# Cluster products of q and k of a group as one piece in two PSUM banks, in a kernel that fuses routed attention with a SwiGLU layer

One Trainium2 chip, one of its cores. The metric is device time in microseconds (us) of one launch; lower is better. All runs that are compared here were at a granted TensorE clock of 0.997 to 1.0. PE is TensorE, DVE VectorE, ACT ScalarE, POOL GpSimd.

## The reference, cut to what matters

```python
def _attn_ref(q, k, v, centroids):             # (4, 8, 768, 64) each; 16 centroids per head
    ...                                        # q_n, k_n, c_n: rows divided by their norms
    q_assign = np.argmax(np.einsum('bhsd,hcd->bhsc', q_n, c_n), axis=-1)
    k_assign = np.argmax(np.einsum('bhsd,hcd->bhsc', k_n, c_n), axis=-1)
    mask = q_assign[:, :, :, None] == k_assign[:, :, None, :]
    scores = np.where(mask, scale * np.matmul(q, k.transpose(0, 1, 3, 2)), -1e9)
    return softmax(scores) @ v                 # written out in the original

def _moe_ref(x, w_gate, w_val, w_out, rms_g):  # x (3072, 512): the attention's output, heads side by side
    xn = x / rms * rms_g
    g = xn @ w_gate                            # (512, 1536)
    return (silu(g) * (xn @ w_val)) @ w_out
```

A query sees only keys of its own cluster. The kernel finds each row's cluster by a product with 16 normalised centroids (the *cluster product*), a maximum and a comparison, and appends the one-hot row of the cluster to q and to k, so that the score matmul itself adds the mask.

## The kernel before: the parts that matter

Work is cut into 8 *units* (half a batch's queries, 8 heads, three *gaps* per head, one after each pair of score matmuls) and 8 *groups* of 4 heads. While ScalarE and TensorE work on the scores of unit u, other work is put between: the SwiGLU products of earlier units and the preparation of a group (u + 2; unit 1 prepares groups 2 and 3). A SwiGLU step is a *gate* product and a *value* product on TensorE, a tanh on ScalarE, and two steps on VectorE (L366 after the gate, L370 after the value) that combine them and so free the two PSUM buffers. All of it goes through engines that take instructions in the program's order.

```python
    ps_s = pool("ps_s", 2, space=PSUM)     # scores, 2 buffers
    ps_a = pool("ps_a", 1, space=PSUM)     # attention output
    ps_g = pool("ps_g", 3, space=PSUM)     # everything else: gate, val, o, transposes, cluster products
...
    def cluster_steps(g, m, h0=0, h1=HG, early=False):       # m: 0 q, 1 k
        ...
        def products(): _products(g, m, h0, h1, early, of)
        def largest():  ...   # DVE: maximum over 16 clusters           (mx)
        def compare():  ...   # DVE: equal to the maximum, bf16         (ohT)
        def back():     ...   # DVE: transpose back to one-hot rows     (oh)
        return [products, largest, compare, back]

    def _products(g, m, h0, h1, early, of):
        ps = ... ps_g.tile([P, UQ], F32, tag="gen", name="sc")
        ...
        for h in range(h0, h1):            # four heads, 32 output columns each, fp32
            nc.tensor.matmul(ps[32 * h:32 * h + 32], lhsT=cblk[:, g * HG % H + h],
                             rhs=qkT[g, h // 2][:, h % 2, m], start=True, stop=True)
        sct = asg.tile([P, UQ], F32, tag="scT", name="scT", bufs=2)
        nc.vector.transpose(sct[r], ps[r])
...
    def group_work(g):
        ...
        a = []
        for m in range(2):
            a += [(0.0 if i else 0.7, f) for i, f in enumerate(cluster_steps(g, m))]
        a.append((0.0, lambda: [place(nc.gpsimd, g, m) for m in range(2)]))
...
    def attention(heads, fill, skip=0, ahead={}, hooks={}):
        gaps = [(u, h, i) for u, h in heads for i in range(UNITS[u][2])]
        total, done, n = sum(c for c, _ in fill), 0.0, 0
        for at, (u, h, i) in enumerate(gaps):
            scores(u, h, i)                # two matmuls into a ps_s buffer, exp on ACT out of it
            ...                            # at i == 1: the value product (acc) of the head before
            if h == H - 1:
                squares(u, i, False)       # ACT: sum of squares of heads 0 to 5, one third per gap of head 7
            ...
            while n < len(fill) and at >= skip and done <= total * (at + 1 - skip) / (len(gaps) - skip):
                done += fill[n][0]         # the cost in us that the author gave the step
                fill[n][1]()
                n += 1
```

With `skip` = 1 the first gap of a unit gets no fill, so that the last score of a unit and the first two of the next stand close together.

The softmax here doesn't subtract the row's maximum and nothing guards it: scores larger than these inputs give would overflow.

Of the kernel before, what the change touches and what calls it, by code (L numbers as in the profile page):

```python
# [22 lines left out]
def kernel(  # L23
# [60 lines left out]
    def load_qk(n):  # L84
        if n < B * H:
            load(n, 0)
            load(n, 1)

    def load_v(n, vq=None):
        if n >= B * H:  # L90
            return
        stagedv[n] = stage.tile([P, ST, D], F32, tag="vs", name="vs", bufs=NV)
        (vq or nc.sync).dma_start(out=stagedv[n], in_=src(v, n))
# [100 lines left out]
    def trans(g, h, part):  # L194
        if (g, h // 2) not in qkT:
            qkT[g, h // 2] = qk32.tile([P, 2, 2, UQ], F32, tag="qkT", name="qkT")
        qk = staged[g * HG + h]
        ps = ps_g.tile([P, UQ], F32, tag="gen", name="tq")
        for i in range(HT):
            nc.tensor.transpose(ps[:, i * P:(i + 1) * P], qk[:, part, 2 * i:2 * i + 2].rearrange("p t d -> p (t d)"),  # L200
                                ident_f)
        nc.scalar.copy(qkT[g, h // 2][:, h % 2, part], ps)  # L202

    def qcast(g, h, es=(0, 1)):
        for e in es:
            nc.gpsimd.tensor_copy(qext[g % 4][:D, h, e * UQ:(e + 1) * UQ], qkT[g, h // 2][e * D:(e + 1) * D, h % 2, 0])  # L206

    def kcast(g, h, on=None, es=(0, 1)):
        for e in es:
            to, of = kext[g % 4][:D, h, e * UQ:(e + 1) * UQ], qkT[g, h // 2][e * D:(e + 1) * D, h % 2, 1]  # L210
            if on is nc.scalar:
                nc.scalar.activation(to, of, ACT.Copy, scale=1.0 / ZS)
            else:
                (on or nc.vector).tensor_scalar_mul(to, of, 1.0 / ZS)  # L214

    def vcast(n):
        nc.gpsimd.tensor_copy(vbf[n // HG % 4][:, n % HG, :, :D], stagedv[n])
# [8 lines left out]
    def cluster_steps(g, m, h0=0, h1=HG, early=False):  # L226

        r = slice(32 * h0, 32 * h1)
        n = UQ // NC
        of = {}  # L230

        def products():
            _products(g, m, h0, h1, early, of)

        def largest():
            of["mx"] = small.tile([P, n], F32, tag="mx", name="mx")
            nc.vector.tensor_reduce(of["mx"][r], of["cl"], axis=AX, op=ALU.max)

        def compare():
            of["ohT"] = asg.tile([P, UQ], BF16, tag="ohT", name="ohT", bufs=2)  # L240
            nc.vector.tensor_tensor(of["ohT"][r].rearrange("p (n c) -> p n c", c=NC), of["cl"],
                                    of["mx"][r].unsqueeze(2).broadcast_to([32 * (h1 - h0), n, NC]), op=ALU.is_equal)

        def back():
            oh = asg.tile([P, UQ], BF16, tag="oh", name="oh", bufs=4)
            nc.vector.transpose(oh[r], of["ohT"][r])  # L246
            put[g, m, h0] = ((kext if m else qext)[g % 4], oh, h0, h1)

        return [products, largest, compare, back]

    def _products(g, m, h0, h1, early, of):
        ps = ps_s.tile([P, UQ], F32, tag="s", name="sc") if early else ps_g.tile([P, UQ], F32, tag="gen", name="sc")
        r = slice(32 * h0, 32 * h1)
        for h in range(h0, h1):
# [4 lines that stand above are left out]
        of["cl"] = sct[r].rearrange("p (n c) -> p n c", c=NC)  # L259
# [3 lines left out]
    def place(on, g, m, h0=0, es=(0, 1)):  # L263

        ext, oh, _, h1 = put[g, m, h0]
        for h in range(h0, h1):
            for e in es:
                on.dma_start(out=ext[D:D + NC, h, e * UQ:(e + 1) * UQ],  # L268
                             in_=oh[32 * h + e * NC:32 * h + (e + 1) * NC])
# [117 lines left out]
    def group_work(g):  # L387

        t, c = [], []
        for h in range(HG):  # L390
            n = g * HG + h
            t += [(0.3, lambda h=h: trans(g, h, 0)), (0.3, lambda h=h: trans(g, h, 1))]

            def casts(h=h, n=n):
                qcast(g, h)
                vcast(n)
                load_qk(n + NQ)
                load_v(n + NV)
                kcast(g, h, es=(0,))
            c += [(0.0, casts), (0.0, lambda h=h: kcast(g, h, es=(1,)))]  # L400
        a = []
        for m in range(2):
            a += [(0.0 if i else 0.7, f) for i, f in enumerate(cluster_steps(g, m))]
        a.append((0.0, lambda: [place(nc.gpsimd, g, m) for m in range(2)]))
        return t, c, a

    def group(g):
        t, c, a = group_work(g)
        return [x for h in range(HG) for x in t[2 * h:2 * h + 2] + c[2 * h:2 * h + 2]] + a
# [13 lines left out]
    def ffn_work(u):  # L423
        n = UNITS[u][2] / HT
        w = [(0.18 * n, lambda c=c: xtrans(u, c)) for c in range(CC)]
        for f in range(FC):
            for val in (False, True):
                w.append((0.64 * n, lambda f=f, val=val: gv(u, f, val)))
        return w

    def out_work(u):
        return [(0.86, lambda t=t, p=p: out_mm(u, t, p)) for t in range(UNITS[u][2]) for p in range(3)]
# [131 lines left out]
    for u in range(1, NU):  # L564
        ffn, o, g = ffn_work(u - 1), out_work(u - 2) if u > 1 else [], u + 2
        if u == 1:
            t, c, a = group_work(2)
            fill, head, prep = [], t, c + a + group(3)
        else:
            fill, head, prep = ffn_work(u - 2)[CUT:], [], group(g) if g < NG else []  # L570
        fill += [(0.0, lambda u=u: rms(u - 1))] + head
        fill += o[:-3] + ffn[:2] + o[-3:-2] + ffn[2:3] + o[-2:-1] + ffn[3:4] + o[-1:] + spread(ffn[CC:CUT], prep)
        attention([(u, h) for h in range(H)], fill, 1)
# [36 lines left out]
```

## Time and profile before

| | before |
|---|---|
| time, median of 3 runs | 361.62 us (361.56 to 361.79) |
| span of the profiled run | 359.7 us |
| busy: PE, ACT, DVE, POOL | 345.2, 256.1, 237.1, 110.2 us |
| two cluster pieces of a group on TensorE, each to the next start, with 0.09 us lost ahead of it | 2 x 0.875 us |

The prediction below shows the lines themselves. One thing helps in reading them: the bracket at the end of a timeline line ("idle before") tells whether the engine stood idle before that instruction, and for whom.

### The profile page before, as it was taken

To read this page: it belongs to the slowest core of one execution; us is meant where nothing else is said; L and a number is where in the kernel's file an instruction comes from. 1 tells how busy PE (TensorE), PEld (TensorE's weight loads), DVE (VectorE), ACT (ScalarE), POOL (GpSimd) and SP (SyncE) were. 2 spreads that over 40 slices of the span, in tenths; PEclk is the share of its full clock that TensorE was granted. 3 is DMA by queue.
4 is the path that set the end of the run, shared out by engine and by line. 5 is a ranking of instruction groups with operands and counts; after the bars stand their busy time and mean duration, and the time that the engine had idled before them with its cause. 6 is when DMAs were issued, how large, how long until landed. Compare 5 with 4: busy or idle time off the path is not lost.

```text
span 359.7 us, 8049 instructions
## 1 busy us (share of the span) xinstructions
PE 345.2 (96%) x3027; PEld 210.0 (58%) x3047; DVE 237.1 (66%) x577; ACT 256.1 (71%) x455; POOL 110.2 (31%) x221
## 2 busy tenths in 40 slices
PE   8999799999999999999999999999999999999995
PEld 4555455655575656755576556756566656654552
DVE  5994379596567874686667865687656575677332
ACT  5789977996588866887588865978668866861320
POOL 1699306896051801535033711327000000000000
PEclk9999999999999999999999999999999999999999
DMA  7549999962154102610130002001010001002002
GB/s 256 185 121 212 244 241 270 334 190 67 64 157 133 24 29 89 202 40 19 59 118 2 16 8 87 2 2 24 38 52 3 0 31 58 2 3 80 8 2 87
DMA packets 28039, 32.03 MB, mean 89 GB/s; under 512 B 4960, under 2 KB 24928, under 8 KB 28000
## 3 DMA queue, kind: packets, MB, share of 16 engines
q1 hardware_dynamic: 18352, 24.75, 21.6%
q0 software_dynamic: 9072, 5.98, 10.0%
q10 hardware_dynamic: 576, 0.79, 0.7%
q8 instruction: 24, 0.39, 0.4%
q14 instruction: 15, 0.12, 0.1%
HBM read 28.35 MB, written 6.29 MB: 96 GB/s over the span
## 4 chain that ended last, share of the span: by engine, by line
PE 71%; DVE 14%; ACT 8%; issue 3%; POOL 1%; DMA 1%; SPq 0%; DVEq 0%; ACTq 0%
PE gate L357 16%; PE val L357 16%; PE s L284 13%; PE o L379 12%; PE acc L302 8%; ACT pT L288 5%; PE tq L200 4%; DVE o_sb L382 2%; PE sc L255 2%; ACT xn L322 2%; DVE xn L334 1%; PE warm L112 1%; DVE th L366 1%; DVE kext L214 1%; DVE scT L258 1%
## 5 line engine op out<-in xcount | busy, mean ns | idle before, releaser
L288 ACT ACTIVATE pT<-s,off 128x768 bf16<-128x768 f32 x192 | 171.0, 902 | 50.2 <-PE s L284 49.1
L284 PE MATMUL s<-qext,kext 80*128 80x384 bf16 x384 | 93.5, 325 | 3.0 <-ACT pT L288 2.6
L357 PE MATMUL gate<-xnT,wg 128*128 128x384 bf16 x384 | 78.5, 325 | 0.2 <-DVE xnT L345 0.2
L357 PE MATMUL val<-xnT,wv 128*128 128x384 bf16 x384 | 78.1, 326 | 0.4 <-DVE th L366 0.3
L366 DVE SCALAR_TENSOR_TENSOR th<-th,gate 128x384 f32<-128x384 f32 x84 | 46.3, 552 | 44.0 <-ACT th L365 43.6
L379 PE MATMUL o<-wo,gvT 128*128 128x512 bf16 x272 | 68.8, 378 | 2.1 <-DVE o_sb L382 1.0
L206 POOL CAST qext<-qkT 64x384 bf16<-64x384 f32 x64 | 33.0, 524 | 93.7 <-ACT qkT L202 92.1
L284 PEld LDWEIGHTS <-kext 80*128 80x128 bf16 x384 | 37.0, 98 | 35.3 <-issue 7.7
L365 ACT ACTIVATE th<-gate 128x384 f32<-128x384 f32 x84 | 41.1, 489 | 15.8 <-PE gate L357 15.2
L357 PEld LDWEIGHTS <-wv 128*128 128x128 bf16 x384 | 36.1, 97 | 26.1 <-issue 4.5
L370 DVE SCALAR_TENSOR_TENSOR gvT<-th,val 128x384 bf16<-128x384 f32 x84 | 46.1, 548 | 7.4 <-PE val L357 2.3
L357 PEld LDWEIGHTS <-wg 128*128 128x128 bf16 x384 | 35.8, 97 | 24.5 <-issue 3.6
L302 PEld LDWEIGHTS <-pT 128*128 128x128 bf16 x1152 | 43.5, 97 | 9.3 <-ACT pT L288 0.6
L302 PE MATMUL acc<-vbf,pT 128*128 128x65 bf16 x1152 | 45.6, 193 | 0.5 <-ACT pT L288 0.5
L379 PEld LDWEIGHTS <-gvT 128*128 128x128 bf16 x288 | 27.0, 97 | 27.7 <-issue 2.0
L202 ACT COPY qkT<-tq 128x384 f32<-128x384 f32 x64 | 29.2, 488 | 5.9 <-PE tq L200 5.0
L200 PE MATMUL tq<-ident_f,qk 128*128 128x128 f32 x192 | 30.2, 280 | 1.6 <-ACT qkT L202 1.2
L268 POOL DMA_DIRECT2D qext<-oh x48 | 23.1, 490 | 24.5 <-DVE oh L246 24.3
L200 PEld LDWEIGHTS tq<-ident_f,qk 128*128 128x128 f32 x192 | 23.2, 143 | 8.7 <-ACT qkT L202 2.2
L214 DVE TENSOR_SCALAR kext<-qkT 64x384 bf16<-64x384 f32 x60 | 23.8, 396 | 2.3 <-ACT qkT L202 1.6
L382 DVE COPY o_sb<-o 128x512 f32<-128x512 f32 x24 | 16.4, 686 | 12.5 <-PE o L379 12.5
L268 POOL DMA_DIRECT2D kext<-oh x48 | 22.9, 485 | 2.4 <-DVE th L366 1.2
(63 smaller groups left out, 241.9 us busy)
## 6 DMA issues: line engine op xcount, KB each, us to landing
qk<-in_q_dram SPq DMA_DIRECT2D x32, 192.0 KB, 3.9
vs<-in_v_dram SPq DMA_DIRECT2D x32, 192.0 KB, 3.7
out_dram<-o_sb SPq DMA_DIRECT2D x24, 256.0 KB, 2.0
qk<-in_k_dram SPq DMA_DIRECT2D x28, 192.0 KB, 4.0
wg<-in_moe_w_gate_dram POOLq DMA_DIRECT2D x4, 384.0 KB, 12.4
wv<-in_moe_w_val_dram POOLq DMA_DIRECT2D x4, 384.0 KB, 14.8
wo<-in_moe_w_out_dram POOLq DMA_DIRECT2D x3, 512.0 KB, 24.7
kext<-oh POOLq DMA_DIRECT2D x52, 12.0 KB, 1.6
```

The lines of the kernel that those rows point to most:

```text
L200: nc.tensor.transpose(ps[:, i * P:(i + 1) * P], qk[:, part, 2 * i:2 * i + 2].rearrange("p t d -> p (t d)"), ident_f)
L202: nc.scalar.copy(qkT[g, h // 2][:, h % 2, part], ps)
L206: nc.gpsimd.tensor_copy(qext[g % 4][:D, h, e * UQ:(e + 1) * UQ], qkT[g, h // 2][e * D:(e + 1) * D, h % 2, 0])
L268: on.dma_start(out=ext[D:D + NC, h, e * UQ:(e + 1) * UQ], in_=oh[32 * h + e * NC:32 * h + (e + 1) * NC])
L284: nc.tensor.matmul(ps[:, j, :w] if nt == HT else flat[:, j * w:(j + 1) * w], lhsT=kext[g % 4][:KR, hh, kc * P:(kc + 1) * P], rhs=qext[g % ...
L288: nc.scalar.activation(pT[u, h][:, n * i:n * i + n, :w], of, ACT.Exp, bias=off, scale=scale * ZS)
L302: nc.tensor.matmul(acc[:, h % 2, t], lhsT=pT[u, h][:, kc, t * P:(t + 1) * P], rhs=vbf[g % 4][:, hh, kc % HT * 2 + kc // HT], start=kc == 0 ...
L357: nc.tensor.matmul(ps, lhsT=w[:, c, f * P:(f + 1) * P], rhs=xnT[u][:, c, :n], start=c == 0, stop=c == CC - 1)
L365: nc.scalar.activation(th, ps, ACT.Tanh, scale=0.5)
L366: nc.vector.scalar_tensor_tensor(th, th, 1.0, ps, op0=ALU.add, op1=ALU.mult)
L370: nc.vector.scalar_tensor_tensor(gvT[u][:, f, :n], gates[u], 0.5, ps, op0=ALU.mult, op1=ALU.mult)
L379: nc.tensor.matmul(outs[u], lhsT=gvT[u][:, f, t * P:(t + 1) * P], rhs=wo[:, f], start=f == 0, stop=f == FC - 1)
```

## The change

The two cluster pieces of a group (q, then k) each take TensorE into its 32-column mode (four products of 32 output columns side by side, in place of one that uses all 128 columns) and out again. The change issues both products in one piece, in two PSUM buffers, to pay for one such excursion per group. DVE's later steps stay single.

```diff
-        a = []
-        for m in range(2):
-            a += [(0.0 if i else 0.7, f) for i, f in enumerate(cluster_steps(g, m))]
+        q_steps, k_steps = (cluster_steps(g, m) for m in range(2))
+        a = [(1.4, lambda: (q_steps[0](), k_steps[0]()))] + [(0.0, f) for f in q_steps[1:] + k_steps[1:]]
         a.append((0.0, lambda: [place(nc.gpsimd, g, m) for m in range(2)]))
```

## The prediction

> **What bounds the kernel now.** I read the page first, then the engines' busy time by stretch, then TensorE's timeline around the cluster products (tile `sc`), then the chain of waits in the stretches where groups are prepared.
>
> The page, parts 1 and 4 (busy time, and the chain that ended last):
>
> ```profile
> PE 345.2 (96%) x3027; PEld 210.0 (58%) x3047; DVE 237.1 (66%) x577; ACT 256.1 (71%) x455; POOL 110.2 (31%) x221
> ...
> PE 71%; DVE 14%; ACT 8%; issue 3%; POOL 1%; DMA 1%; SPq 0%; DVEq 0%; ACTq 0%
> ```
>
> TensorE (PE) is busy 96% and carries 71% of the chain. So time taken off TensorE's stream shortens the run, unless it is taken where VectorE (DVE) or ScalarE (ACT) set the pace, and 22% of the chain is theirs. Where is that? The windows view answers for two stretches, first the one in which groups 2 and 3 are prepared (attention of unit 1), then a piece of unit 3, which stands for units 2 to 5 (groups 4 to 7, one each):
>
> ```profile
> 50.00:60.00 10.00, 9.91 (x96) 5.33 (x95) 9.46 (x22) 7.89 (x12) 3.01 (x6) 1.00 1.16 267
> 60.00:70.00 10.00, 9.67 (x110) 7.32 (x108) 6.81 (x17) 9.30 (x17) 8.39 (x17) 1.00 1.11 327
> 70.00:80.00 10.00, 9.70 (x98) 5.36 (x94) 9.05 (x19) 9.07 (x18) 9.13 (x19) 1.00 0.66 198
> ...
> 110.50:119.50 9.00, 9.00 (x90) 4.88 (x88) 7.49 (x17) 6.86 (x15) 2.87 (x7) 1.00 0.22 67
> ```
>
> The columns after the length are PE, weight loads, DVE, ACT and GpSimd. In unit 1 DVE has 9.46 of 10 us while the cluster steps of group 2 run and 9.05 while those of group 3 run, with ACT at 9.07: three engines are nearly full. In the later unit PE is full and DVE and ACT have a fifth free. The chain of waits, asked for these stretches alone, agrees: from 108 to 121 us every piece of it is PE; from 49.8 to 64.1 and from 71.5 to 80.3 us nearly every piece is DVE, ending in these two:
>
> ```profile
> 64.09 0.81 PE val L357 x4
> ...
> 80.35 0.81 PE val L357 x4
> ```
>
> Both are value products that waited for DVE's gate step to free a PSUM buffer.
>
> **What one piece of cluster products costs TensorE.** The timeline of PE in unit 3 (start us, duration, what); the ends of matmuls are modelled, so I use differences of starts only:
>
> ```profile
> 111.19 0.49 PE L284 MATMUL s<-qext,kext 80*128 80x384 bf16 x2
> 111.61 0.85 PE L255 MATMUL sc<-qkT,cblk 128*32 128x384 f32 x8
> 112.40 0.50 PE L357 MATMUL val<-xnT,wv 128*128 128x384 bf16 x2
> ```
>
> A score matmul of 384 columns holds PE about 0.163 us start to start (two in sequence 0.325), so the score pair ends its stream at 111.52. The cluster product starts at 111.61: about 0.09 us of nothing. Then the next matmul starts 0.79 us after it (0.785 in the records). The eight records are four 32-column products of two passes each; the second pass of a product follows the first at about 0.35, the four products of a pass within 0.02. Two passes of 384 columns[...] are 2 x 0.32 = 0.64 us. So one piece takes 0.09 + 0.785 = 0.875 us, of which about 0.23 is neither streaming nor anything else.
>
> **What the Trainium skill says.**
> - "TensorEngine Tiling (Array Packing)", Tiling Modes, Key Properties: "Changing tiling mode (not just tile) drains the TensorE". The cluster products are 128x32 tiles between 128x128 matmuls, so each piece has two such changes. The trace agrees in size: 0.09 us before, and about 0.1 us after the last stream.
> - "Perfetto Trace Analysis", Tensor Engine Instruction: the profiler's matmul end is computed, not observed. Agreed: PE's records overlap (0.49 us for two that take 0.325). Hence a "busy" of 9.00 of 9.00 does not mean that there is no idle time to win, and I count starts.
> - "Perfetto Trace Analysis", Optimizing Tensor Performance, Matmuls: independent groups should rotate through PSUM banks so that evacuation overlaps. Here three buffers rotate among transposes, gate, value and cluster products, and the change fills two of the three at once. The two waits at 64.09 and 80.35 show that this rotation already bites in unit 1.
>
> **The change, part by part.** Nothing is added or removed: the same eight cluster matmuls per group, the same transposes (0.57 us each), reductions, comparisons and transposes back on DVE. For groups 2 to 7 the products of k move up beside those of q, and the transposes of the two PSUM tiles stand back to back; the built order shows `sc x8` where `sc x4` stood twice, once in unit 2 to 5 each and twice in unit 1. Groups 0 and 1 are untouched.
>
> *Removed:* one entry and one exit of the tiled mode per group. The kernel before contains the merged form once already, in its prologue, where two half pieces follow each other directly:
>
> ```profile
> 11.28 0.38 PE L112 MATMUL warm<-kext 128*128 128x512 bf16 x1
> 11.59 1.48 PE L255 MATMUL sc<-qkT,cblk 128*32 128x384 f32 x8
> 13.01 0.55 PE L200 MATMUL tq<-ident_f,qk 128*128 128x128 f32 x3
> ```
>
> Next start minus first start is 1.42 us (1.415) for four passes; a lone half piece of two passes at 9.20 us takes 0.77. A second pair of passes thus costs 1.415 - 0.771 = 0.644 us: pure streaming. So the merged piece should take 0.785 + 0.644 + 0.09 = 1.52 us in place of 2 x 0.875 = 1.75: **0.23 us saved per group**.
>
> *Units 2 to 5 (4 groups):* is the saving kept? I walked the new order with the durations above, from the cluster piece's start at t = 0. Its q bank is written by about 0.75, its k bank by 1.4. DVE transposes them by about 1.4 and 2.1. The order of PE afterwards is two scores, gate, two scores, 18 of the `acc` products, value, gate, two scores, value. The gate at 1.75 needs the bank of the value product before the piece (freed about 0.6), the value at 3.4 needs the q bank (1.4), the gate at 4.1 the k bank (2.1), the next value at 5.1 needs the first gate's bank, freed by DVE's gate step at about 3.8. Every bank is free over a microsecond ahead, so no new wait. One small stall of the old kernel stays: in the old trace the value after the second piece starts at 117.59, 0.16 us late, and the third of four scores 0.07 late. That sum is set by ACT (tanh 0.49, then exp 0.9, before a score buffer is free), so freeing the value's bank earlier only moves it to the score. Saved: 4 x 0.23 = **0.92 us**, all on PE's path.
>
> *Unit 1 (2 groups):* the PE time is saved too, 2 x 0.23 = 0.46, but here DVE paces. The gate after the merged piece of group 2 reaches PE at about 55.24 and needs the bank that DVE frees at 55.43 (`gvT` at 54.89, 0.55 long), so it starts at about 55.48: a wait of 0.24 eats the saving. Later DVE does two transposes, a maximum and two gate steps in another order; by summing its steps from 55.73 I get the second gate step done at about 61.9 against 61.2 before, and the transposes of q that need its bank would wait some 0.5 us. The value that waited until 64.09 would then start between 63.8 and 64.4. For group 3 DVE and ACT are both full and the same set of DVE steps precedes the gate step that releases the value at 80.35. I set unit 1 at **0, give or take 0.5**.
>
> Sum: 361.62 - 0.92 - 0 = **360.7 us**, 0.25% less.
>
> **The rivals.**
> 1. *All of it arrives* (also in unit 1): 6 x 0.23 = 1.4, plus two small waits of the old order in group 2 that would vanish (0.13 before the second piece, 0.18 before a transpose): about 360.0. For it: PE is 97 to 99% busy in unit 1 as well, and DVE has some idle pieces there that the new order may fill. Against it: the chain there is DVE's.
> 2. *A PSUM wait takes the place of the switch.* Two of three buffers are held until two transposes of DVE are through, 1.1 us plus DVE's queue. If DVE lags by over a microsecond in the later units as well, each group gains a wait of 0.2 to 0.5 us: 361 to 362.5. For it: DVE is 83% busy in the window at 110.5, and its order is fixed. Against it: my walk leaves over a microsecond.
> 3. *ACT starves, then is late.* During 1.52 us no score is made, and afterwards four scores come close together (group 3). ACT has 24% free in the later unit and each exp takes 0.9; in unit 1 this could cost 0.5 once: 361.2.
> 4. *Off the path.* If the unit boundaries (exp, squares, then DVE's normalisation) set the time, nothing changes: 361.6. Against it: PE waits for almost nothing between 85 and 125.
>
> **Range and chances.** The core, 0.92, rests on a measured merged piece and is good to 0.15; unit 1 adds 0.5 either way, and rival 2 has perhaps one chance in seven. The runs before agree within 0.25 us. So 8 times in 10 the time is between 359.8 and 361.7. Two per cent would be 7.2 us; all the cluster products' own PE time in these groups is 6 x 1.75 = 10.5, so neither side is within reach: faster 0.01, same 0.98, slower 0.01.
>
> **What would show it.** Right: each merged piece has 16 records and the next matmul starts about 1.43 us after the first; from unit 2 to unit 5 the distance between the same score matmul of successive units shrinks by about 0.23; DVE, ACT and PE do as many instructions as before. In unit 1 a gate waits for `gvT` just after the piece, and a transpose of q some 4 us later. Wrong: a gap over 0.2 us on PE after the piece in units 2 to 5 with DVE's `scT` as releaser (rival 2), over 0.6 us gained in unit 1 (rival 1) or lost there (rivals 2 and 3), or a merged piece longer than 1.6 us, which would make the switch cheaper than I take it.

## The result, and the profile after

| | before | after |
|---|---|---|
| time, median of 4 runs each | 361.59 us | 362.25 us |
| span of the profiled run | 359.7 us | 360.3 us |

The ratio is 1.0029, 95% interval 1.0004 to 1.0053: not faster by 0.25% but slower by 0.3%. (A ratio here is the mean time of one kernel's fast runs over that of the other's of the same rounds, so not quite the ratio of the medians.) 362.25 lies above the predicted range, whose top was 361.7.

The page of the kernel after, parts 1 and 4:

```profile
PE 344.4 (96%) x3047; PEld 210.0 (58%) x3047; DVE 236.4 (66%) x577; ACT 256.2 (71%) x455; POOL 109.5 (30%) x221
...
PE 65%; ACT 11%; DVE 10%; DMA 6%; POOL 3%; issue 3%; SPq 0%; ACTq 0%; POOLq 0%; DVEq 0%
```

The work is the same (the 20 PE records more are some that the first trace had lost), but PE carries less of the chain and ACT more, 11% against 8%. That is the first hint.

The merged piece itself is what was forecast. PE's timeline in unit 2 (the stretch from 108 to 119 us that the prediction calls unit 3; counted by exps, three per head, it is the end of unit 2, and the reading is the same):

```profile
112.18 0.81 PE L357 MATMUL val<-xnT,wv 128*128 128x384 bf16 x4
112.92 1.50 PE L255 MATMUL sc<-qkT,cblk 128*32 128x384 f32 x16
114.36 0.50 PE L284 MATMUL s<-qext,kext 80*128 80x384 bf16 x2
```

The next matmul starts 1.43 us after the first of sixteen records, in all six merged pieces, and 0.09 us are lost ahead of it: 1.52 us, as worked out, and 0.23 less than two pieces. So the saving was made. Where did it go?

To find out I take the start of the exp of each head (the ACT instruction on L288) in both traces, count from the first exp of unit 1, and subtract:

| exp of (unit, head) | after minus before, us |
|---|---|
| 1,4 | -0.15 |
| 1,5 | +0.43 |
| 1,7 and 2,0 | +1.05, +1.04 |
| 2,2 to 2,6 | +1.05 |
| 2,7 | +1.72 |
| 3,0 | +1.01 |
| 4,0; 5,0; 6,0 | +1.00, +0.99, +0.98 |
| end of the run | +1.01 |

(Unit 1 itself starts at 40.11 us in one trace and at 39.69 in the other; the kernels are the same until there, and this start lay between 39.69 and 40.90 in the runs. That is as wide as the scatter of one kernel's times, 362.05 to 363.13 for the kernel after; counting from there takes it out of the comparison.)

So all of the loss, 1.04 us, arises in unit 1. In units 2 to 5 nothing is lost and next to nothing gained: 0.06 for four groups in place of 0.92. And in each of them the exp of head 7 is suddenly 0.68 later, and back by the next unit.

**Units 2 to 5.** ACT's timeline around head 7 of unit 2, before:

```profile
113.64 0.90 ACT L288 ACTIVATE pT<-s,off 128x768 bf16<-128x768 f32 x1 [0.97 <-PE s L284]
...
115.32 0.90 ACT L288 ACTIVATE pT<-s,off 128x768 bf16<-128x768 f32 x1
...
117.30 0.49 ACT L365 ACTIVATE th<-gate 128x384 f32<-128x384 f32 x1 [0.58 <-PE gate L357]
117.69 0.89 ACT L288 ACTIVATE pT<-s,off 128x768 bf16<-128x768 f32 x1
```

and after:

```profile
114.95 0.90 ACT L288 ACTIVATE pT<-s,off 128x768 bf16<-128x768 f32 x1 [1.62 <-PE s L284]
115.75 0.51 ACT L322 ACTIVATE xn<-x 128x384 bf16<-128x384 f32 x1
...
116.26 0.48 ACT L365 ACTIVATE th<-gate 128x384 f32<-128x384 f32 x1
116.63 0.90 ACT L288 ACTIVATE pT<-s,off 128x768 bf16<-128x768 f32 x1
...
117.91 0.49 ACT L365 ACTIVATE th<-gate 128x384 f32<-128x384 f32 x1
118.28 0.91 ACT L288 ACTIVATE pT<-s,off 128x768 bf16<-128x768 f32 x1
```

Read the brackets. Before, ACT stood idle 0.97 us ahead of head 7's first exp, and again 0.58 us ahead of a tanh: it kept up and waited for PE. After, it stands idle 1.62 us while PE does the merged piece, and from 114.95 on no line has a bracket: ACT works without a break through exp, squares (L322), tanh, exp, squares, tanh, exp. It is behind, and PE finds it so. PE's timeline, before and then after:

```profile
117.59 0.81 PE L357 MATMUL val<-xnT,wv 128*128 128x384 bf16 x4
118.23 0.88 PE L284 MATMUL s<-qext,kext 80*128 80x384 bf16 x4
```

```profile
117.85 0.81 PE L357 MATMUL val<-xnT,wv 128*128 128x384 bf16 x4
118.50 0.49 PE L284 MATMUL s<-qext,kext 80*128 80x384 bf16 x2
119.25 0.48 PE L284 MATMUL s<-qext,kext 80*128 80x384 bf16 x2 [0.26 <-ACT pT L288]
```

Four score matmuls in a row are the last score of unit 2 and the first of unit 3. The second pair needs a score buffer whose exp is not finished. By differences of starts (118.50 to 119.25, where two score matmuls take 0.325) PE loses 0.42 us there; before, it lost 0.07 there and 0.16 at the value product ahead. The account of a unit: 0.23 less for the mode, 0.16 less at the value, 0.35 more at the score, together -0.04; measured -0.01 to -0.03.

**Unit 1.** The windows view of the kernel after, for the three stretches that the prediction shows of before:

```profile
50.00:60.00 10.00, 9.68 (x96) 5.62 (x95) 9.73 (x23) 7.95 (x12) 3.49 (x7) 1.00 1.17 267
60.00:70.00 10.00, 9.24 (x107) 7.00 (x106) 6.92 (x16) 8.80 (x16) 8.36 (x17) 1.00 1.10 325
70.00:80.00 10.00, 8.90 (x93) 4.96 (x90) 8.07 (x18) 8.72 (x17) 9.50 (x20) 1.00 0.73 218
```

PE's busy time fell from 9.91, 9.67 and 9.70 of 10 us. Its timeline names what it waited for:

```profile
59.30 0.81 PE L357 MATMUL val<-xnT,wv 128*128 128x384 bf16 x4 [0.26 <-DVE gvT L370]
...
61.65 0.81 PE L357 MATMUL gate<-xnT,wg 128*128 128x384 bf16 x4 [0.31 <-DVE th L366]
...
64.22 0.81 PE L357 MATMUL val<-xnT,wv 128*128 128x384 bf16 x4 [0.45 <-DVE th L366]
...
77.58 0.48 PE L284 MATMUL s<-qext,kext 80*128 80x384 bf16 x2 [1.09 <-ACT pT L288]
```

Before, the last two were at 64.09 and 76.95, with brackets of 0.33 and 0.30; the first two have no counterpart. At group 2's piece PE waits for DVE to free PSUM buffers; group 3's loses time to ACT at the same kind of place as in the later units. There the merged piece holds back head 7's first score by 0.64 us, which is the second product's share of it (1.43 less 0.785). ACT's timeline of the kernel before shows why none of it was made good:

```profile
72.00 1.94 ACT L288 ACTIVATE pT<-s,off 128x768 bf16<-128x768 f32 x2 [0.51 <-PE s L284]
...
79.65 0.90 ACT L288 ACTIVATE pT<-s,off 128x768 bf16<-128x768 f32 x1 [0.28 <-PE s L284]
```

No line between these two has a bracket, and from 72.10 to 78.80 ACT is busy 6.56 of 6.70 us: in unit 1 it had next to no idle time in head 7 even before the change.

### The profile page after: what moved, and what is told of

The parts are those of the page before. It is cut to its first block, busy times and chain, and to the rows that moved or that the text cites. A ratio compares the mean times of both kernels' runs of the same rounds, so it can differ in the third digit from the quotient of the medians.

```text
span 360.3 us, 8076 instructions
## 1 busy us (share of the span) xinstructions
PE 344.4 (96%) x3047; PEld 210.0 (58%) x3047; DVE 236.4 (66%) x577; ACT 256.2 (71%) x455; POOL 109.5 (30%) x221
## 4 chain that ended last, share of the span: by engine, by line
PE 65%; ACT 11%; DVE 10%; DMA 6%; POOL 3%; issue 3%; SPq 0%; ACTq 0%; POOLq 0%; DVEq 0%
PE val L357 14%; PE gate L357 14%; PE o L379 12%; PE s L284 11%; ACT pT L288 7%; PE acc L302 7%; PE tq L200 4%; DMA vs<-in_v_dram 4%; ACT xn L322 3%; DVE o_sb L382 2%; DMA qext<-oh 2%; PE sc L255 2%; POOL qext L206 1%; PE warm L112 1%; ACT th L365 1%
## 5 line engine op out<-in xcount | busy, mean ns | idle before, releaser
L288 ACT ACTIVATE pT<-s,off 128x768 bf16<-128x768 f32 x192 | 171.0, 903 | 55.2 <-PE s L284 54.2
L379 PE MATMUL o<-wo,gvT 128*128 128x512 bf16 x288 | 70.0, 379 | 1.3 <-DVE o_sb L382 1.0
L200 PE MATMUL tq<-ident_f,qk 128*128 128x128 f32 x192 | 30.4, 277 | 1.6 <-ACT qkT L202 1.2
L200 PEld LDWEIGHTS tq<-ident_f,qk 128*128 128x128 f32 x192 | 22.9, 141 | 8.2 <-ACT qkT L202 2.2
L214 DVE TENSOR_SCALAR kext<-qkT 64x384 bf16<-64x384 f32 x60 | 23.0, 383 | 2.7 <-ACT qkT L202 1.6
```

Of the source, the lines that this page charges most:

```text
L200: nc.tensor.transpose(ps[:, i * P:(i + 1) * P], qk[:, part, 2 * i:2 * i + 2].rearrange("p t d -> p (t d)"), ident_f)
L288: nc.scalar.activation(pT[u, h][:, n * i:n * i + n, :w], of, ACT.Exp, bias=off, scale=scale * ZS)
L379: nc.tensor.matmul(outs[u], lhsT=gvT[u][:, f, t * P:(t + 1) * P], rhs=wo[:, f], start=f == 0, stop=f == FC - 1)
```

## The experiments

**Theory A (ScalarE).** The merged piece holds back the next score. ACT's idle time there cannot be made up, since head 7 gives it the squares as well; PE then waits for ACT where scores stand close together. **Theory B (PSUM).** The piece fills two of three buffers, and PE waits for DVE to empty them. **Theory C (order).** Removing one step shifts the others among the gate and value products, and DVE's new order costs. Each kernel below was correct and was timed in 5 rounds beside the kernel before on the same chip. "Unit 1" is the shift of exp (2,2), the first that all the variants of a unit's start have behind them; "per unit" is a quarter of the change from (2,2) to (6,4), which holds units 2 to 5. Both are read as in the table above, against the profile of before: the kernel after has +1.05 and -0.01.

Unit 1 scatters: kernels whose code is the same as before's up to (2,2) read -0.13 (m47), -0.12 (m47_sk) and -0.45 (before_sk) there, and before_sq and m47_sq_sk, which share their code that far, +0.49 and +0.03. So one figure of unit 1 carries up to half a microsecond, and I build on it only where several agree. Units 2 to 5 are steady: the four steps of one kernel agree within 0.02 or 0.03.

### Where it is lost: only the later groups, only the early groups

```diff
+        if g >= 4:       # m47; in m23: if g <= 3
+            (merged, as in the change)
+        else:
+            (as before)
```

> Cluster products merged only for groups 4 to 7 (units 2 to 5); groups 2 and 3 as before. Theory (ScalarE: the merged piece holds back the scores of the last head, ScalarE then works without a break and the third of four scores waits for it): the 0.23 us saved per group is taken back by a longer wait of that score, 0.42 instead of 0.23, so unit 2 to 5 gain 0.02 to 0.05 each and the time is before minus 0.1, ratio 0.9997. My prediction's own claim for these units: minus 0.92, ratio 0.9975. If the loss seen came from the later units, it would be over 1.0015.

Measured: median 361.35 us, before 361.60; ratio 0.9991 (0.9975 to 1.0007). Unit 1 -0.13, per unit 0.00, the whole -0.13 from unit 1 on. The exp of head 7 comes 0.68 later and is back by the next unit.

> Merged only for groups 2 and 3 (unit 1). Theory: all of the loss is here, plus 1.0 us, ratio 1.003, of it 0.4 by the fifth head of unit 1 (group 2) and 0.6 after it (group 3). Rival (the loss is spread or is the noise of runs): under plus 0.4 us, ratio under 1.001.

Measured: median 362.72, ratio 1.0030 (1.0012 to 1.0049). Unit 1 +0.77, and nothing afterwards. At head 5 it is +0.13 (+0.43 in the kernel after), at head 7 +0.77: group 3's 0.64 repeats (0.62 in the kernel after), group 2's part does not.

So the whole loss is unit 1's, and in units 2 to 5 the saving is offset almost exactly. Both theories A and B could still do that.

### Is it ScalarE? The squares moved into its idle time, with and without the merge

```diff
-            if h == H - 1:
+            if 1 <= u <= 5:
+                if (h, i) == (H - 2, UNITS[u][2] - 1):
+                    squares(u, 0, False)
+                    squares(u, 1, False)
+                if (h, i) == (H - 1, 0):
+                    squares(u, 2, False)
+            elif h == H - 1:
                 squares(u, i, False)
```

> The changed kernel with the squares of heads 0 to 5 moved ahead in ScalarE's order in units 1 to 5: two to just after the last exp of head 6, where ScalarE stands idle during the merged piece (1.62 us in unit 3), the third to the first gap of head 7. Theory (ScalarE's backlog): the wait of 0.42 us at the third of four scores goes in units 2 to 5 and that of 1.26 us in unit 1 shrinks by 0.7 or so; 362.25 minus 4 x 0.45 minus 0.7 = about 359.7. Rival (PSUM buffers held by the cluster products, or VectorE's order, are what costs): no change from the changed kernel, 362.2.

Measured: median 361.77, ratio 1.0001 (0.9983 to 1.0018). Per unit -0.16; the wait at the third score fell from 0.42 to 0.23. Unit 1: +0.66 against +1.05. The time missed the expectation by 2 us, because only a part of the wait went. ACT's timeline of this kernel says why:

```profile
113.53 0.52 ACT L322 ACTIVATE xn<-x 128x384 bf16<-128x384 f32 x1
...
115.26 0.90 ACT L288 ACTIVATE pT<-s,off 128x768 bf16<-128x768 f32 x1 [0.61 <-PE s L284]
...
118.03 0.49 ACT L365 ACTIVATE th<-gate 128x384 f32<-128x384 f32 x1 [0.19 <-PE gate L357]
```

The squares now lie in the idle time, and ACT has a bracket again ahead of the last tanh: it is no longer behind. What is left, 0.23 us, is no backlog. It is a chain: the gate product ends, then tanh, then the exp that was issued behind it, then the score buffer is free.

> The kernel before with the same move of the squares: the control. Theory: its waits at the third of four scores and at the value ahead of it (0.23 together) go in units 2 to 5, and 0.4 at the same place of unit 1: 361.6 minus 0.9 minus 0.4 = about 360.3, so that the merge is then worth minus 0.9 in units 2 to 5 and plus 0.4 in unit 1. Rival (the squares' place does not matter without the merge): 361.6.

Measured: median 361.77, ratio 1.0003 (0.9988 to 1.0018). Per unit +0.01: the waits of 0.16 and 0.07 stayed. Unit 1 reads +0.49. My expectation was wrong, and the trace of before had shown it: ACT stood idle 0.58 us ahead of that tanh, so it had no backlog to relieve.

The pair together: the same move gains 0.16 per unit with the merge and nothing without. The merge made a backlog on ACT, which is theory A. Theory B predicted no change. Unit 1 agrees from head 6 to (2,2), the stretch of group 3: the merge costs 0.64 there without the move (0.41 to 1.05 in the kernel after) and 0.11 with it (0.45 in after_sq less 0.34 in before_sq; m47_sq_sk, the same code there without the merge, reads 0.39), while kernels with unit 1 as before read +0.01 to -0.24. The move itself costs 0.34 to 0.39 there, so it is no remedy.

### Is the saving there at all? Other work where TensorE waits

One gate product goes between the last unit's final score and the second score of the next unit, that is, into the unit's first gap:

```diff
+            if at == 0 and u in (3, 4, 5, 6):     # sk27: 2 to 7; sk26: 2 to 6
+                done += fill[n][0]
+                fill[n][1]()
+                n += 1
             while n < len(fill) and at >= skip and done <= ...
```

> Groups 4 to 7 merged, and in units 3 to 6 one gate product is put between the first two scores of the unit, where the profile shows the wait for ScalarE (the third of four scores in a row). Theory (TensorE's saving is only waited away at that one place): with other work to do there TensorE keeps most of it; against the kernel before, units 2 to 5 gain 0.25 to 0.45 each, minus 1.0 to 1.8 in all. Rival (ScalarE bounds the whole unit, so any gain is waited for at the next score): units gain under 0.05 each, time as of m47.

Measured: median 359.69, before 361.74; ratio 0.9942 (0.9924 to 0.9959). Per unit -0.42, the whole -1.82 from unit 1 on. PE's timeline at the boundary of units 3 and 4:

```profile
159.04 0.49 PE L284 MATMUL s<-qext,kext 80*128 80x384 bf16 x2
159.37 0.81 PE L357 MATMUL gate<-xnT,wg 128*128 128x384 bf16 x4
160.02 0.49 PE L284 MATMUL s<-qext,kext 80*128 80x384 bf16 x2
```

No bracket, and starts 0.33 and 0.65 apart, which is the plain length of the work. ACT is still behind here, but nobody waits for it.

> The control: the kernel before with the gate product between the first two scores of units 3 to 6. It can gain only what TensorE waits there without the merge, 0.07 at the score and perhaps the 0.16 at the value before it: 0.07 to 0.23 each, minus 0.3 to 0.9 in all. If it gains as much as m47_sk, the merge itself is worth nothing even when ScalarE is fed.

Measured: median 361.07, ratio 0.9982 (0.9965 to 0.9999). Per unit -0.05; the wait of 0.16 at the value product is still there. (The whole is -0.65, but 0.45 of it arose in unit 1, whose code is as before: scatter.) So the gate product alone is worth 0.05, and the merge on top of it 0.37: the 0.23 of the mode and most of the 0.16 at the value product, whose buffer is freed earlier in the merged order.

> The same with the squares moved ahead as well (units 1 to 5). Theory: no wait over 0.1 us is left after the merged piece in units 2 to 5, so the whole 0.23 of the merge and the 0.23 that TensorE waited in the kernel before are gained: minus 0.45 each, minus 1.8 in units 2 to 5; unit 1 loses 0.5 as it did in the control. Rival: minus 0.16 each as with the squares alone.

Measured: median 359.71, ratio 0.9951 (0.9932 to 0.9970). Per unit -0.43, as without the moved squares. Unit 1 reads +0.03, where I expected the +0.5 of before_sq, whose code it shares there: scatter. With work at the boundary the squares' place no longer matters.

### An earlier place for the piece

```diff
-        fill += ... + spread(ffn[CC:CUT], prep)
+        fill += ... + (spread(ffn[CC:CUT - 4], prep) + ffn[CUT - 4:CUT])     # units 2 to 5; groups 4 to 7 merged
```

> Groups 4 to 7 merged, with the group's work spread over 12 of the 16 gate and value products instead of all, so that the merged piece stands in head 6, ahead of the scores of head 7 with their squares. Theory (it is the place just before ScalarE's busiest stretch that spoils it): ScalarE has caught up by head 7, the wait at the third score is back at 0.2, and 0.15 to 0.25 are gained per unit, minus 0.6 to 1.0 in all. Rival (a merged piece starves ScalarE wherever it stands): no gain, as m47; or a new wait of DVE or PSUM appears in the denser stretch, a loss.

Measured: median 363.17, ratio 1.0038 (1.0019 to 1.0057). The wait at the third score was back at 0.23 as theory A says, but per unit 0.43 was *lost*: in unit 3 PE waited 0.39 us for DVE's gate step at a value product and 0.27 for ACT's copy at another, in the stretch that now holds the same preparation in three quarters of the products. So the place did what it should, and the rival of the expectation, a new wait in the denser stretch, came true. No kernel without the merge was run in this order, so how the loss divides is open.

### Is unit 1 a matter of shifted places?

```diff
-        a = [(1.4, both products)] + [(0.0, f) for f in q_steps[1:] + k_steps[1:]]
+        a = [(0.7, both products)] + [(0.0, f) for f in q_steps[1:]]
+        a += [(0.7, lambda: None)] + [(0.0, f) for f in k_steps[1:]]      # groups 2 to 7
```

> All groups 2 to 7 merged, but with an empty step of the same weight left where the products of k stood, so that every other step keeps its place among the gate and value products. If the losses come from the shifted places of the other steps (VectorE's order in unit 1, the missing fill between two scores in group 3), unit 1 is now near the kernel before (plus 0.3 at most). In units 2 to 5 ScalarE's backlog should still eat the saving, because the score of head 7 still comes 0.65 us later: 0 to minus 0.1 each. In all 361.3 to 361.9. Rival (back-to-back transposes and two held PSUM buffers cost by themselves): unit 1 loses 0.8 or more as in m23.

Measured: median 362.10, before 361.62; ratio 1.0020 (1.0008 to 1.0032). Unit 1 +0.69, and +0.93 at (2,0), so theory C fails as the main cause. All profiles say the same at (2,0), where no boundary product has acted yet (kernels with the squares as before): the two with this order read +0.93 and +0.77, the three with the order of the change (after, m23, after_sk26) +1.04, +0.77 and +0.73, and those with groups 2 and 3 single -0.21 to +0.22. The order makes no difference there; the merge costs about 0.9. The extra wait of the gate product at 61.65 did go with the old order, and at head 5 this kernel is only +0.06; but between heads 6 and 7 it lost the same 0.64, and PE waited 0.88 us at the third score. Units 2 to 5 lost 0.05 each: the wait there was 0.43 again.

> The same with a gate product between the first two scores of units 2 to 7. Theory: units 2 to 5 keep 0.4 each as in m47_sk, the end of unit 6, where the kernel before waits 0.42 for ScalarE too, gives 0.3 more, unit 1 stays within 0.3: minus 1.6 to 2.3, about 359.5. If the boundary of unit 1 was what group 3 lost, minus 2.3 rather than minus 1.6.

Measured: median 359.22, ratio 0.9944 (0.9930 to 0.9958). Unit 1 -0.03, per unit -0.40, and the end of unit 6 gained 0.42: the whole -2.03.

> The changed kernel as it is, with a gate product between the first two scores of units 2 to 6. Theory: group 3 lost 0.6 at the third of four scores (1.26 us of waiting for ScalarE in place of 0.46), so much of it comes back at the start of unit 2, and units 2 to 5 gain 0.4 each; group 2 keeps its loss of 0.1 to 0.4: minus 1.3 to 1.9 against the kernel before. Rival (in unit 1 VectorE's order is the bound, so the wait only moves): unit 1 keeps plus 0.8 to 1.0, minus 0.7 in all.

Measured: median 360.51, ratio 0.9974 (0.9960 to 0.9988). Unit 1 +0.48, per unit -0.43, the whole -1.24. The gate product took 0.57 off unit 1's figure here, but it took 0.65 off without the merge as well (m47 -0.13, m47_sk27 below -0.78). So this does not show that the merge's loss in unit 1 was the wait at the boundary: with the boundary filled in both kernels, the one that merges groups 2 and 3 as well is still 1.26 later by these two profiles (+0.48 against -0.78).

### The version that beats both

> Groups 4 to 7 merged, gate product between the first two scores of units 2 to 7: m47_sk with the starts of units 2 and 7 added. Theory: the wait of 0.42 at the start of unit 7 and of 0.46 at that of unit 2, both for ScalarE, fill up with work: minus 0.2 to 0.8 more than m47_sk, so minus 2.0 to 2.6. Rival: those two waits come back at the next score, minus 1.8 as m47_sk.

Measured: median 358.30, before 361.62; ratio 0.9919 (0.9906 to 0.9932), that is 0.8% faster. Unit 1 -0.78, per unit -0.40, end of unit 6 -0.42: the whole -2.82 from unit 1 on. Merged where ACT and DVE have room, single in unit 1, and one product of other work at each unit's start. Against pad_sk27, which merges everywhere and was timed in the same rounds, it is 0.25% faster by the two ratios, and unit 1 differs by 0.75 (-0.78 against -0.03): merging groups 2 and 3 costs even so. This kernel merges in units 2 to 5 only, so the merge's own part of the -2.82 is about 4 x 0.35 = 1.4 (0.40 less the 0.05 of before_sk). The other half is the gate product's and unit 1's scatter; no control without any merge had the gate product at the starts of units 2 and 7.

## Why the prediction was wrong

- **The cost of a switch: right.** 0.23 us per group was forecast from the prologue's merged piece; the six pieces take 1.43 us to the next start and 1.52 with the entry, to 0.01. The prediction put the loss down to the mode and did not name a rival, the change of number type from bf16 to fp32. The trace of before speaks for the mode: in the prologue an fp32 transpose on all 128 columns (L200) is followed after 0.109 us by the next fp32 one and equally by a bf16 matmul, but, in the one place where it happens, after 0.203 by a cluster product, which is fp32 too.
- **"Saved: 4 x 0.23 = 0.92 us, all on PE's path": this step failed.** The walk through the new order asked, for every PE instruction, whether its PSUM buffer of the gate-and-value pool would be free; it was right there, and no such wait appeared in units 2 to 5. It did not walk ACT. It took the old wait of 0.16 + 0.07 as fixed ("That sum is set by ACT"), as if ACT could begin its tanh whenever the gate product ended. But moving k's products up delays the first score of head 7 by 0.68, and the bracket of 0.58 ahead of the last tanh, which I could have read in the old trace, was all the slack that ACT had after it. The wait became 0.42 and the gain 0.01 to 0.03 per unit. after_sq against before_sq shows that 0.19 of the 0.42 was ACT's backlog, and what stayed is the chain of tanh and exp; m47_sk against before_sk shows that the saving can be had.
- **Rival 3 was right in kind and too small in reach.** I gave it only to unit 1 ("this could cost 0.5 once") because ACT has 24% free in the later unit. The average over 9 us hid that in head 7 each gap brings ACT an exp and a square, and two of the three a tanh as well.
- **Unit 1, "0, give or take 0.5": wrong in size.** It lost 1.04. Group 2's waits came about as forecast (the gate after the piece: 0.23 of 0.24; a wait for the second gate step: 0.47 of 0.5, though at a gate product in place of a transpose), and at head 5 the six kernels with group 2 merged read +0.06 to +0.43 (mean 0.18) where the eight with it single, before among them at 0, read -0.32 to +0.11 (mean -0.19): a loss of about 0.4. Group 3 is what I missed: 0.62 to 0.64, mainly at the third of four scores, where PE's wait for ACT grew from 0.46 to 1.26 us, because ACT had next to no idle time in head 7 to take the delay. I had argued that the same set of DVE steps precedes the value product at 80.35; The loss had arisen before that one, where PE waited for ACT.
- **Rival 2 was wrong for the later units** and part of group 2's story in unit 1. How group 2's loss divides between buffers held and DVE's order is not settled: the two order-preserving kernels read +0.06 and +0.22 at head 5, the four others +0.11 to +0.43, which is within the scatter of unit 1.
- **Rival 4 (off the path): wrong as put.** Unit boundaries do not hide the gain for good; one wait there did, and work put into it brought it out.

The Trainium skill states the rule that makes the wait what it is: "TensorE: Matmul & The Clock Gate", Architectural detail, has ACT and DVE as strict first-in first-out queues. The traces agree: the exp at 118.28 stands behind the tanh at 117.91, although its score product (117.52, 0.49 long in the profile) had ended at about 118.0, and PE's next score waits for that exp.

## What to carry to other kernels

When a change gathers work of the bounding engine into one piece, ask not only whether its own buffers are free but what the piece holds back: for every engine that it feeds, read the idle brackets in the stretch after it, and take the delay off that slack before counting the saving. If the slack is used up, look for the one place where the bounding engine then waits, and put independent work there; here that turned 0.01 per unit into 0.4. And merge only where the neighbours have room: the same piece, with that work in place, gained in units 2 to 5 and lost in unit 1.

## What the Trainium skill lacked or had wrong

- "TensorEngine Tiling (Array Packing)", Tiling Modes, Key Properties, says that a change of mode drains TensorE, with no figure. Here 0.09 us went on the way in, and one excursion less per group saved 0.23 us in all (2 x 0.875 against 1.52).
- "Trainium Kernel Development and Optimization", Best Practices, says, of judging the distance to the roofline, that for engines other than TensorE occupancy is fine; it does not say that occupancy misses when a delay turns such an engine into the bound. Here ACT's occupancy of 71% over the span, and of 76% over the 9 us around head 7 of the kernel before, did not tell that 0.68 us of delay would make it the bound for 4 us; the 0.58 us of idle time left ahead of its last tanh did.
- "Perfetto Trace Analysis", Matmuls, asks for rotation over PSUM banks so that evacuation overlaps. That was kept here and was not enough in units 2 to 5: with every buffer of that pool free, filling two at once still moved 0.35 us of waiting to the score buffers, through ACT. No page tells to check the consumers of the work that a longer piece delays.
